# A fused attention and expert kernel: the next batch's keys split three steps sooner, and a new hand-over to the experts

## The chip, the cores and the metric

The kernel runs on one core of a Trainium2 chip. TensorE (PE) does the matrix products, VectorE (DVE) and ScalarE (ACT) prepare their operands and empty their sums, GpSimd (POOL) issues the row scatters, and SyncE (SP) issues the loads. The metric is the device time of one execution in microseconds, the median of several runs.

## The reference

`u`, `v` are 8 x 2496 x 256, `z` is 8 x 2496 x 64, and there are 8 experts with a hidden width of 1024. Everything is float32.

```python
scores = (1.0 / S) * np.matmul(z, z.transpose(0, 2, 1))     # per batch, S = 2496
attn = np.maximum(scores, 0.0) ** 2
x = (u * np.matmul(attn, v)).reshape(N, D)                  # N = 19968 tokens, D = 256
logits = x @ w_gate + modality_bias[modality_id]
e_idx = np.argmax(logits, axis=1)                           # one expert per token
gate_w = softmax(logits)[arange(N), e_idx]
out[mask_e] = gate_w * (np.maximum(x[mask_e] @ w1[e], 0.0) @ w2[e])
```

## The kernel before, in words

**Precision.** Every float32 operand of a product is split into a high part (rounded to the format that PE takes) and a low part (operand minus high), and the product is the sum of three: high x high, high x low, low x high. ACT or DVE rounds the high parts (`zm` L220, `vh` L234, `ah` L280, `hh` L954); DVE alone subtracts for the low parts (`zm` L225, `vl` L240, `al` L289, `hl` L955).

**Attention.** Each batch has five chunks of queries (four of 512 and one of 448) and twenty blocks of 128 keys. A step `g` is one chunk of queries with two blocks of keys: 10 steps to a chunk, 50 to a batch, 400 in all. `scores` (L265) puts two blocks' products into the tile `s`, which exists once (two PSUM banks); ACT takes `s` through a relu into `r` (L267) and squares it (L273); `high` and `low` split it; `weigh` (L305) adds its product with `v` to the sums `acc`. Scores run four steps ahead of `weigh` once the pipe is full, so `scores(g)` stands on PE in step `g - 4`. The fifth chunk's keys of a batch that starts at step `g0` are first read by `scores(g0 + 8)`, hence in step `g0 + 4`. When a chunk of queries ends, ACT copies half of its sums out (`evacuate_low`, L347), DVE adds the other half (`evacuate_high`, L351), PE turns the result into rows (`make_rows`, tile `po`, L363), DVE multiplies by `u` (`take_rows`, L373), and 32 DVE products per chunk make the gate's logits (L385).

**What sets the order.** PE, ACT, DVE and POOL run their instructions in the order in which the program writes them. A planner writes it: `at(g, f)` puts a task right behind step `g`; `queue(g, end, pieces)` lets pieces wait from step `g` on until an account of ACT's and DVE's time has room, and at step `end` at the latest; a second piece follows one step later. Loads go through SP's queue, in which an instruction that waits for a buffer holds up those behind it. `z` is loaded into three raw buffers (`zr`), which the subtraction at L225 frees.

**Hand-over and experts.** The tokens of the early batches are already sorted into expert queues in memory (`scatter`, L496 and L498), so four expert tiles of 512 tokens can run before the last tokens are routed. In a tile, `up` makes eight slices of the hidden layer (tile `ph`, six matmuls, L950), ACT and DVE split each (`hh`, `hl`), and `down` (L963, L964) multiplies slice `f - 2` with the second weights behind slice `f`; slices 6 and 7 follow at the tile's end. `finish` empties the four sums with ACT (`part2`, L978) and DVE (`y`, L980). The rest of the last batch's work (turning the last chunk, its logits, the routing of its 12 late columns, the plan for all other tiles) is hung into the first four tiles by the table `between[tile][slice]`. `route_count` (L462) is a product on PE that reads `cnt` (L453) of `route_places`. Phase one's PSUM holds `s` in its first two banks and six banks that `acc`, `po` and others share; phase two's pools lie over the same banks in the order in which they are opened, and a tile waits for the users of the bank under it.

Of the kernel before, what the change touches and what calls it, by code (L numbers as in the profile page):

```python
# [15 lines left out]
P = 128  # L16
# [10 lines left out]
def tile_attention_moe(ctx: ExitStack, tc: tile.TileContext, u, v, zt, mid, wg, mb, w1, w2, out):  # L27
# [11 lines left out]
    nc = tc.nc  # L39
# [138 lines left out]
    nc.sync.dma_start(out=brow, in_=mb.rearrange("(o m) e -> o m e", o=1).broadcast_to([P, 2, E]))  # L178
    mod = [small.tile([P, B, NCOL, 1], F32, name=f"mod{i}") for i in range(2)]

    def load_modality():
        mi = raw.tile([P, B, NCOL, 2], I32, tag="mi", name="mi")
# [73 lines left out]
    def scores(g):  # L256
# [4 lines left out]
        for n, (kl, ql) in enumerate(((0, 1), (1, 0), (0, 0))):  # L261
            for t in range(2):
                k = 2 * i + t
                lhs = Z[b, k // J][halves[t], kl, (k % J) * P:(k % J + 1) * P]
                nc.tensor.matmul(out=s[:, t, :w], lhsT=lhs, rhs=mv[halves[t], ql, :w], start=n == 0, stop=n == 2)  # L265
# [391 lines left out]
    for b in range(B):  # L657
        g0 = b * per
        if b:
            for c in range(NCH):  # L660
# [4 lines left out]
                queue(gz, g0 + 2 * c - 5, act(0.6, prep_z_high, b, c), dve(0.7, prep_z_low, b, c))  # L665
                queue(gv, g0 + 2 * c - 2, act(1.05, prep_v_high, b, c), dve(1.25, prep_v_low, b, c))
        for c in range(NCH):
# [4 lines left out]
            for h in reversed(range(KD)):  # L672
                queue(g + NI, g, dve(0.7, evacuate_high, b, c, h))
            if b < B - 1 or c < NCH - 1:
                at(g + NI, make_rows, b, c)
# [159 lines left out]
    with tc.manual_schedule(engines={ET.PE, ET.Activation, ET.DVE, ET.Pool}):  # L835
# [88 lines left out]
        assert not tasks  # L924
        waiting += [(end, g, p) for g in sorted(due) for end, p in due[g]]
# [5 lines left out]
    ph2 = ctx.enter_context(ExitStack())  # L931
    bank.update(pool=ph2.enter_context(tc.tile_pool(name="ps_m", bufs=2, space=PSUM, reuse_waits="tile")), tag="m")
# [3 lines left out]
    ps_h = ph2.enter_context(tc.tile_pool(name="ps_h", bufs=2, space=PSUM, reuse_waits="tile"))  # L936
# [95 lines left out]
    for n in range(LGN):  # L1032
        between[0][1 + n * (KF - 1) // LGN].append(lambda n=n: logits(B - 1, NCH - 1, n))
    planning = plan()
    slots = [(n, f) for n in range(EARLY) for f in range(KF)]
    late = slots[KF:]
    for (n, f), pieces in zip(late, ((route_logits, route_exp), (route_places,), (route_count,), (route_slots, route_gates))):
        between[n][f] += [lambda p=p: p(B - 1, LATE) for p in pieces]
    for k, (n, f) in zip(range(LATE.start, NCOL), late[4:]):
        between[n][f].append(lambda k=k: scatter(B - 1, k))  # L1040
    for n, f in late[3:8]:
        between[n][f] += [lambda: next(planning, None)] * 2
    n, f = late[7]
# [65 lines left out]
```

## Time and profile before

| what | value |
|---|---|
| time, median of 3 runs | 2329.91 us (2325.26 to 2331.11) |
| the profiled execution's own time | 2333.17 us |
| its span, first to last instruction | 2330.9 us |
| TensorE busy | 2280.6 us, 98% |
| VectorE busy | 1758.5 us, 75% |
| ScalarE busy | 1588.7 us, 68% |
| mean granted TensorE clock | 0.990 |

The span is what the trace covers; the execution's own time has 2.27 us around it. A granted clock of 1.0 is 2.4 GHz and 0.5 is 1.2 GHz. Busy shares are averages over the attention phase (to about 1387 us) and the expert tiles behind it.

### The profile page before, as it was taken

The numbers are of one execution on the slowest core, as the hardware profiler recorded it, in microseconds if no ns is written. First come the engines' busy times: TensorE is split into PE (matmuls) and PEld (weight loads), VectorE is DVE, ScalarE is ACT, GpSimd is POOL, SyncE is SP. The second block draws the span as 40 slices with busy tenths as digits, with TensorE's granted clock in tenths as the row PEclk, the third lists the DMA queues.
The fourth block names the chain that finished last, engine by engine and source line by source line (L and its number), as shares of the span: only waits on it lengthen the run. The fifth ranks groups of instructions, "written<-read, shape, count | busy, mean of one in ns | idle before, by whom it ended". The sixth has DMA issues, their size and how long they took to land.

```text
span 2330.9 us, 44748 instructions
## 1 busy us (share of the span) xinstructions
PE 2280.6 (98%) x17220; PEld 2069.5 (89%) x17220; DVE 1758.5 (75%) x4539; ACT 1588.7 (68%) x1967; POOL 366.3 (16%) x350
## 2 busy tenths in 40 slices
PE   9999999999999999999999999999999999999996
PEld 7888998998998998998998987888888888888885
DVE  6879988988988888988888987555656565656563
ACT  7888887888887887888888862454545454545453
POOL 0000210210210220220210412221211111111211
PEclk9999999999999999999999999999999999999998
DMA  9602112112112112112110122343434343434340
GB/s 299 221 28 67 47 48 67 45 48 75 38 52 70 40 51 69 40 59 61 51 40 30 62 90 80 128 154 118 161 111 162 112 162 112 160 116 156 124 144 24
DMA packets 101790, 216.88 MB, mean 93 GB/s; under 512 B 15488, under 2 KB 63104, under 8 KB 96704
## 3 DMA queue, kind: packets, MB, share of 16 engines
q1 hardware_dynamic: 86432, 172.61, 22.5%
q0 software_dynamic: 15136, 41.34, 4.8%
q8 instruction: 136, 2.23, 0.4%
q14 instruction: 86, 0.70, 0.1%
HBM read 168.36 MB, written 62.32 MB: 99 GB/s over the span
## 4 chain that ended last, share of the span: by engine, by line
PE 89%; DVE 6%; issue 2%; ACT 2%; DMA 0%; POOL 0%; DVEq 0%; ACTq 0%; POOLq 0%
PE acc L305 40%; PE ph L950 18%; PE po L963 12%; PE s L265 11%; PE po L964 6%; DVE spare L385 2%; DVE al L289 1%; PE pt L794 1%; PE po L363 1%; ACT r L267 1%; ACT r L273 0%; DVE ah L280 0%; DVE x L373 0%; DVE x L351 0%; DVE hl L955 0%
## 5 line engine op out<-in xcount | busy, mean ns | idle before, releaser
L267 ACT ACTIVATE r<-s 128x1024 f32<-128x1024 f32 (+1 forms) x400 | 403.5, 1009 | 224.8 <-PE s L265 219.0
L289 DVE TENSOR_TENSOR al<-r,ah 128x1024 fp32r<-128x1024 f32 (+1 forms) x360 | 431.1, 1198 | 127.7 <-ACT ah L280 112.2
L305 PE MATMUL acc<-ah,vh 64*128 64x512 f32 (+1 forms) x3120 | 474.4, 386 | 0.9 <-DVE ah L280 0.9
L305 PE MATMUL acc<-ah,vl 64*128 64x512 f32 (+1 forms) x3120 | 466.9, 385 | 0.0
L305 PE MATMUL acc<-al,vh 64*128 64x512 f32 (+1 forms) x3120 | 463.4, 383 | 0.0
L385 DVE SCALAR_TENSOR_TENSOR spare<-x,wgb 128x256 f32<-128x256 f32 x1280 | 462.4, 421 | 1.2
L954 ACT ACTIVATE hh<-ph 128x512 fp32r<-128x512 f32 (+1 forms) x320 | 189.7, 593 | 391.1 <-PE ph L950 377.7
L963 PE MATMUL po<-w,hh 128*128 128x512 f32 x1264 | 454.2, 394 | 0.0
L950 PE MATMUL ph<-xh,w 128*128 128x512 f32 (+1 forms) x1280 | 448.1, 396 | 3.6 <-DVE x L351 3.1
L273 ACT ACTIVATE r<-r 128x1024 f32<-128x1024 f32 (+1 forms) x400 | 416.2, 1040 | 3.5
L955 DVE SCALAR_TENSOR_TENSOR hl<-ph,hh 128x512 fp32r<-128x512 f32 (+1 forms) x320 | 219.1, 685 | 264.2 <-ACT hh L954 260.7
L265 PE MATMUL s<-zm 64*128 64x512 f32 (+1 forms) x2400 | 372.5, 390 | 21.9 <-DVE zm L225 19.2
L305 PEld LDWEIGHTS acc<-ah,vh 64*128 64x128 f32 x3120 | 363.5, 186 | 18.7 <-ACT x L347 1.7
L305 PEld LDWEIGHTS acc<-ah,vl 64*128 64x128 f32 x3120 | 362.1, 186 | 15.6
L305 PEld LDWEIGHTS acc<-al,vh 64*128 64x128 f32 x3120 | 363.3, 185 | 14.1
L498 POOL DMA_INDIRECT xs<-x,sloti x160 | 204.8, 1280 | 1063.4 <-DVE x L496 967.4
L964 PE MATMUL po<-w,hl 128*128 128x256 f32 x1264 | 354.4, 280 | 3.3 <-DVE hl L955 3.3
L265 PEld LDWEIGHTS s<-zm 64*128 64x128 f32 x2400 | 270.3, 186 | 37.4 <-DVE zm L225 23.0
L280 ACT CAST ah<-r 128x1024 fp32r<-128x1024 f32 (+1 forms) x292 | 297.1, 1017 | 0.0
L950 PEld LDWEIGHTS ph<-xh,w 128*128 128x128 f32 x1280 | 240.4, 188 | 60.2 <-DVE x L351 3.5
L963 PEld LDWEIGHTS po<-w,hh 128*128 128x128 f32 x1264 | 238.1, 188 | 55.5
L982 POOL DMA_INDIRECT out_dram<-y,ids x158 | 154.1, 975 | 727.6 <-DVE y L980 702.9
(138 smaller groups left out, 1972.0 us busy)
## 6 DMA issues: line engine op xcount, KB each, us to landing
w<-w1s SPq DMA_DIRECT2D x37, 1024.0 KB
w<-w2s SPq DMA_DIRECT2D x37, 1024.0 KB
xg<-xs SPq DMA_DIRECT2D x39, 516.0 KB
vr<-in_v_dram SPq DMA_DIRECT2D x32, 512.0 KB
ut<-in_u_dram SPq DMA_DIRECT2D x32, 512.0 KB
zr<-in_zt_dram SPq DMA_DIRECT2D x40, 256.0 KB
w1s<-in_moe_w_dram SPq DMA_DIRECT2D x8, 1024.0 KB
w2s<-in_moe_w_dram SPq DMA_DIRECT2D x8, 1024.0 KB
```

The source lines that it names most:

```text
L265: nc.tensor.matmul(out=s[:, t, :w], lhsT=lhs, rhs=mv[halves[t], ql, :w], start=n == 0, stop=n == 2)
L267: nc.scalar.activation(out=r[:, :, :w], in_=s[:, :, :w], func=AF.Relu, scale=INV)
L273: nc.scalar.square(out=a[:, :, :w], in_=a[:, :, :w])
L280: copy(out=ah[:, :, :w], in_=st_a[g][:, :, :w])
L289: nc.vector.tensor_tensor(out=al[:, :, :w], in0=a[:, :, :w], in1=ah[:, :, :w].bitcast(F32), op=ALU.subtract)
L305: nc.tensor.matmul(out=acc[b, c][r][dh][:, :w], lhsT=V[b, k // J][y][halves[r], k % J, dh * P:(dh + 1) * P], rhs=x[halves[r], k % 2, :w], ...
L385: nc.vector.scalar_tensor_tensor(out=spare[:, k % 2, :], in0=x[:, j, 0:D], scalar=1.0, in1=wgb[:, e, :], op0=ALU.mult, op1=ALU.mult, accum ...
L498: nc.gpsimd.indirect_dma_start(out=xs, out_offset=bass.IndirectOffsetOnAxis(ap=RT[b]["sloti"][:n, k:k + 1], axis=0), in_=x[:n, j, :], in_o ...
L950: nc.tensor.matmul(out=ph, lhsT=lhs, rhs=rhs[:, k, :], start=n == 0, stop=n == 3 * KD - 1)
L955: nc.vector.scalar_tensor_tensor(out=hl, in0=ph, scalar=0.0, in1=hh.bitcast(F32), op0=ALU.max, op1=ALU.subtract)
L963: nc.tensor.matmul(out=po[j], lhsT=hh[:, s], rhs=both, start=f == 0, stop=False, skip_group_check=True)
L964: nc.tensor.matmul(out=po[j][:, 0:D], lhsT=hl[:, s], rhs=w[:, 0, :], start=False, stop=f == KF - 1, skip_group_check=True)
```

## The change

Five edits:

- `prep_z_high` and `prep_z_low` of a later batch have to be written three steps sooner (`g0 + 2 * c - 8` in place of `- 5`).
- The last chunk's `evacuate_high` leaves the planner's queue and is written right behind the last step, ahead of what is left in that queue.
- The pool of `ph` is opened first in phase two, so its two banks are those that `s` had; the general pool `m` gets the next two, which `ph` had.
- In the table `between`, the last logits are spread over slices 1 to 6 in place of 1 to 7; `route_logits` goes from the second tile's slice 0 to the first tile's slice 7, `route_places` from slice 1 of the second tile to slice 0, `route_count` and `route_slots` stay at slices 2 and 3, the scatters stay, and the plan's eight pieces run one to a slice from the second tile's slice 4 in place of two to a slice from its slice 3. The load of the next weights, which needs the plan, goes from slice 7 of the second tile to slice 4 of the third.
- The gate's bias (`brow`) is loaded behind the first `z` and `v` and not ahead of them, and the very first scores take the product of the high parts first.

```diff
-    nc.sync.dma_start(out=brow, in_=mb.rearrange("(o m) e -> o m e", o=1).broadcast_to([P, 2, E]))
     def load_modality():
+        nc.sync.dma_start(out=brow, in_=mb.rearrange("(o m) e -> o m e", o=1).broadcast_to([P, 2, E]))
...
-        for n, (kl, ql) in enumerate(((0, 1), (1, 0), (0, 0))):
+        for n, (kl, ql) in enumerate(((0, 1), (1, 0), (0, 0)) if g else ((0, 0), (0, 1), (1, 0))):
...
-                queue(gz, g0 + 2 * c - 5, act(0.6, prep_z_high, b, c), dve(0.7, prep_z_low, b, c))
+                queue(gz, g0 + 2 * c - 8, act(0.6, prep_z_high, b, c), dve(0.7, prep_z_low, b, c))
...
-            for h in reversed(range(KD)):
-                queue(g + NI, g, dve(0.7, evacuate_high, b, c, h))
             if b < B - 1 or c < NCH - 1:
+                for h in reversed(range(KD)):
+                    queue(g + NI, g, dve(0.7, evacuate_high, b, c, h))
...
         assert not tasks
+        for h in reversed(range(KD)):
+            evacuate_high(B - 1, NCH - 1, h)
         waiting += [(end, g, p) for g in sorted(due) for end, p in due[g]]
...
+    ps_h = ph2.enter_context(tc.tile_pool(name="ps_h", bufs=2, space=PSUM, reuse_waits="tile"))
     bank.update(pool=ph2.enter_context(tc.tile_pool(name="ps_m", bufs=2, space=PSUM, reuse_waits="tile")), tag="m")
...
-    ps_h = ph2.enter_context(tc.tile_pool(name="ps_h", bufs=2, space=PSUM, reuse_waits="tile"))
...
-        between[0][1 + n * (KF - 1) // LGN].append(lambda n=n: logits(B - 1, NCH - 1, n))
+        between[0][1 + n * (KF - 2) // LGN].append(lambda n=n: logits(B - 1, NCH - 1, n))
...
-    slots = [(n, f) for n in range(EARLY) for f in range(KF)]
-    late = slots[KF:]
-    for (n, f), pieces in zip(late, ((route_logits, route_exp), (route_places,), (route_count,), (route_slots, route_gates))):
+    slots = [(n, f) for n in range(EARLY) for f in range(KF)][KF - 1:]
+    for k, pieces in ((0, (route_logits, route_exp)), (1, (route_places,)), (3, (route_count,)), (4, (route_slots, route_gates))):
+        n, f = slots[k]
         between[n][f] += [lambda p=p: p(B - 1, LATE) for p in pieces]
-    for k, (n, f) in zip(range(LATE.start, NCOL), late[4:]):
+    for k, (n, f) in zip(range(LATE.start, NCOL), slots[5:]):
         between[n][f].append(lambda k=k: scatter(B - 1, k))
-    for n, f in late[3:8]:
-        between[n][f] += [lambda: next(planning, None)] * 2
-    n, f = late[7]
+    for n, f in slots[5:13]:
+        between[n][f].append(lambda: next(planning, None))
+    n, f = slots[13]
     between[n][f] += [lambda: fetch_weights(0)]
```

The changed file is two lines longer, so from the hand-over on its line numbers are two higher (L957 of the changed kernel is L955 of the one before).

ScalarE where the second batch begins, right behind the copies of the first batch's last sums (`zm` is the fifth chunk's high part). Before:

```order
L347 COPY x<-acc 128x448 x2
L234 CAST vh<-vr 128x1024
L267 ACTIVATE r<-s 128x1024
L273 ACTIVATE r<-r 128x1024
L267 ACTIVATE r<-s 128x1024
L280 CAST ah<-r 128x1024
L273 ACTIVATE r<-r 128x1024
L234 CAST vh<-vr 128x1024
L267 ACTIVATE r<-s 128x1024
L273 ACTIVATE r<-r 128x1024
L220 CAST zm<-zr 128x512
```

Now:

```order
L347 COPY x<-acc 128x448 x2
L234 CAST vh<-vr 128x1024
L220 CAST zm<-zr 128x512
L267 ACTIVATE r<-s 128x1024
L273 ACTIVATE r<-r 128x1024
L267 ACTIVATE r<-s 128x1024
L273 ACTIVATE r<-r 128x1024
L234 CAST vh<-vr 128x1024
L267 ACTIVATE r<-s 128x1024
```

The rounding of `zm` moved up past three relus, three squares and a rounding of `v`, and the rounding of `ah` (L280) that stood there left ScalarE for VectorE. The other six batch starts read alike.

VectorE at the same place, from a low part of `v` on (`zm` is the fifth chunk's low part). Before:

```order
L240 TENSOR_TENSOR vl<-vr,vh 128x1024
L289 TENSOR_TENSOR al<-r,ah 128x1024
L373 TENSOR_TENSOR x<-po,ut 128x4x2x64 x2
L280 CAST ah<-r 128x1024
L289 TENSOR_TENSOR al<-r,ah 128x1024
L385 SCALAR_TENSOR_TENSOR spare,lg<-x,wgb 128x256 x6
L240 TENSOR_TENSOR vl<-vr,vh 128x1024
L289 TENSOR_TENSOR al<-r,ah 128x1024
L385 SCALAR_TENSOR_TENSOR spare,lg<-x,wgb 128x256 x2
L225 TENSOR_TENSOR zm<-zr,zm 128x512
```

Now:

```order
L240 TENSOR_TENSOR vl<-vr,vh 128x1024
L225 TENSOR_TENSOR zm<-zr,zm 128x512
L280 CAST ah<-r 128x1024
L289 TENSOR_TENSOR al<-r,ah 128x1024
L373 TENSOR_TENSOR x<-po,ut 128x4x2x64 x2
L280 CAST ah<-r 128x1024
L289 TENSOR_TENSOR al<-r,ah 128x1024
L385 SCALAR_TENSOR_TENSOR spare,lg<-x,wgb 128x256 x2
L240 TENSOR_TENSOR vl<-vr,vh 128x1024
```

The subtraction of `zm` moved up past three of `al`, one of `vl`, eight logits, the two of `take_rows` and one rounding.

VectorE at the hand-over, from the last two low parts of the first weights on (`x<-acc` is `evacuate_high`). Before:

```order
L774 TENSOR_TENSOR w_0_18681<-w_0_18681 128x4x256 x2
L496 COPY x<-side 128x2
L385 SCALAR_TENSOR_TENSOR spare,lg<-x,wgb 128x256 x2
L351 TENSOR_TENSOR x<-acc,x 128x448 x2
L955 SCALAR_TENSOR_TENSOR hl<-ph,hh 128x512 x2
```

Now:

```order
L774 TENSOR_TENSOR w_0_18681<-w_0_18681 128x4x256 x2
L351 TENSOR_TENSOR x<-acc,x 128x448 x2
L496 COPY x<-side 128x2
L385 SCALAR_TENSOR_TENSOR spare,lg<-x,wgb 128x256 x2
L957 SCALAR_TENSOR_TENSOR hl<-ph,hh 128x512 x2
```

The two additions moved ahead of one copy and two logits. PE's order is the same in both kernels.

## Rows read from the trace of the kernel before

**Rows 1.** The page: busy times, and one of the costliest groups (busy, mean ns).
```profile
PE 2280.6 (98%) x17220; PEld 2069.5 (89%) x17220; DVE 1758.5 (75%) x4539; ACT 1588.7 (68%) x1967; POOL 366.3 (16%) x350
...
L385 DVE SCALAR_TENSOR_TENSOR spare<-x,wgb 128x256 f32<-128x256 f32 x1280 | 462.4, 421 | 1.2
```

**Rows 2.** TensorE's waits: us in total, times, longest.
```profile
PE s L265 <- DVE zm L225: 19.2, 8, 2.7
PE po L964 <- DVE hl L955: 3.3, 2, 2.9
```

**Rows 3.** Timeline of TensorE, 34 to 201 us: start, duration, work, [idle before <- releaser].
```profile
34.38 0.74 PE L265 MATMUL s<-zm 64*128 64x512 f32 x4 [0.58 <-DVE zm L225]
...
201.03 0.73 PE L265 MATMUL s<-zm 64*128 64x512 f32 x4 [2.24 <-DVE zm L225]
```

**Rows 4.** Windows of 7 us behind three z waits; PEclk stands right behind POOL.
```profile
201.03:208.03 7.00, 7.00 (x48) 5.61 (x50) 3.60 (x7) 3.29 (x4) 0.00 (x0) 0.76 0.41 133
373.43:380.43 7.00, 7.00 (x36) 5.58 (x38) 3.60 (x7) 2.10 (x3) 0.00 (x0) 0.57 0.40 118
...
1063.88:1070.88 7.00, 7.00 (x62) 5.75 (x64) 4.40 (x8) 4.88 (x5) 0.00 (x0) 1.00 0.44 135
```

**Rows 5.** Timeline of VectorE, 189 to 209 us.
```profile
189.66 1.22 DVE L240 TENSOR_TENSOR vl<-vr,vh 128x1024 fp32r<-128x1024 f32 x1
...
200.28 0.69 DVE L225 TENSOR_TENSOR zm<-zr,zm 128x512 fp32r<-128x512 f32 x1
...
208.83 1.23 DVE L289 TENSOR_TENSOR al<-r,ah 128x1024 fp32r<-128x1024 f32 x1 [4.09 <-ACT ah L280]
```

**Rows 6.** Timeline of ScalarE, 186 to 195 us.
```profile
186.83 1.05 ACT L267 ACTIVATE r<-s 128x1024 f32<-128x1024 f32 x1
...
194.76 0.60 ACT L220 CAST zm<-zr 128x512 fp32r<-128x512 f32 x1
```

**Rows 7.** Timeline of TensorE, 187 to 188 us.
```profile
187.93 0.50 PE L265 MATMUL s<-zm 64*128 64x512 f32 x1
```

**Rows 8.** Timeline of TensorE at the hand-over and in the first two tiles.
```profile
1389.77 0.79 PE L950 MATMUL ph<-xh,w 128*128 128x512 f32 x1 [3.13 <-DVE x L351]
...
1392.63 0.94 PE L363 MATMUL po<-ident,x 64*128 64x64 f32 x16
...
1413.12 0.28 PE L964 MATMUL po<-w,hl 128*128 128x256 f32 x1
...
1423.28 0.27 PE L462 MATMUL pc<-cnt,below 128*128 128x8 f32 x1 [1.94 <-DVE cnt L453]
...
1444.09 0.38 PE L964 MATMUL po<-w,hl 128*128 128x256 f32 x1 [2.89 <-DVE hl L955]
```

**Rows 9.** Windows of 7 us behind the hand-over's three long waits, of which one stands.
```profile
1389.77:1396.77 7.00, 7.00 (x37) 5.30 (x38) 2.11 (x4) 1.36 (x3) 0.00 (x0) 0.76 0.29 94
```

**Rows 10.** Timeline of VectorE at the hand-over.
```profile
1386.00 2.35 DVE L774 TENSOR_TENSOR w<-w 128x1024 fp32r<-128x1024 f32 x2
...
1389.10 1.15 DVE L351 TENSOR_TENSOR x<-acc,x 128x448 f32<-128x448 f32 x2
```

**Rows 11.** Timeline of VectorE, the first tile's last low part.
```profile
1411.97 0.69 DVE L955 SCALAR_TENSOR_TENSOR hl<-ph,hh 128x512 fp32r<-128x512 f32 x1 [0.26 <-ACT hh L954]
```

**Rows 12.** Timeline of TensorE at the start.
```profile
6.33 1.35 PE L265 MATMUL s<-zm 64*128 64x512 f32 x6
```

**Rows 13.** Timeline of VectorE at the start.
```profile
5.41 0.69 DVE L225 TENSOR_TENSOR zm<-zr,zm 128x512 fp32r<-128x512 f32 x1 [3.68 <-ACT zm L220]
```

**Rows 14.** Timeline of SP: a load of z, and the load of weights that needs the plan.
```profile
162.37 0.33 SPq L215 DMA_DIRECT2D zr<-in_zt_dram  x1
...
1444.56 0.34 SPq L750 DMA_DIRECT2D w<-w1s  x1
```

**Rows 15.** Window of 4 us behind that load; DMA share and GB/s are last.
```profile
1456.00:1460.00 4.00, 4.00 (x22) 3.40 (x21) 1.53 (x4) 0.62 (x2) 1.08 (x2) 1.00 0.16 55
```

**Rows 16.** Timeline of ScalarE: the first use of those weights.
```profile
1476.41 1.04 ACT L770 CAST w<-w 128x1024 fp32r<-128x1024 f32 x1
```

## The prediction

> **What bounds the kernel now.** I read the page first. TensorE is busy 98% of the span, no other engine over 75% [rows 1], so only what TensorE waits for, or runs at half clock, can be won. TensorE's waits come next: the largest is scores (L265) waiting for VectorE's low part of z (L225), eight times and 19.2 us, and layer two's matmul (L964) waits 3.3 us for hl [rows 2]. TensorE's timeline places them. One of the eight is the 0.58 us at 34.38 in the first batch; the other seven are one at each later batch's start, of 2.24 us at the first and of 2.71 to 2.74 us at the six others, 18.6 us in all [rows 2, 3]. At each it is the scores that read the fifth chunk's keys.
>
> The windows behind these seven waits show a second price. In the 7 us behind the first wait TensorE was granted 0.76 of full speed, so it ran at 1.2 GHz for part of it, and 7 x (1 - 0.76) = 1.7 us of work was lost. Three others are like it (0.76 to 0.78), the second one lost 7 x 0.43 = 3.0 us, and the last two read 1.00 and lost nothing [rows 4]. Together 6.5 + 3.0 = 9.5 us.
>
> VectorE's timeline says why z is late: the subtraction at 200.28 stands at the end of a queue that VectorE works off without a gap, while the low part of v at 189.66 stood eleven microseconds before. Behind it VectorE has nothing to do for 4.09 us before 208.83 [rows 5]. So the batch start is a matter of order, not of VectorE's sum of work.
>
> The hand-over has the other waits: 3.13 us before the first expert matmul at 1389.77, for the last sums; 1.94 us before route_count at 1423.28, for cnt; 2.89 us (3.3 with a second) at 1444.09, for hl behind the plan [rows 2, 8]. The 7 us behind each of the three read 0.76, as in the one shown: 1.7 us lost each [rows 9].
>
> **z three steps sooner.** No instruction is added. By the order of VectorE the subtraction now stands right behind the low part of v of 189.66, so it starts at 189.66 + 1.22 = 190.9, when the scores need it at 201.03 - 2.24 = 198.8: seven microseconds to spare [rows 3, 5]. Gain: 18.6 us of waits and the 9.5 us of half clock behind them, 28.1 us. What is late next: on VectorE everything between the new and the old place moves back by 0.69 us, and by as much again for the rounding of ah that comes over from ScalarE; the 4.09 us gap takes both.
>
> On ScalarE the rounding (0.60 us [rows 6]) now stands ahead of a relu that is itself just in time: that relu runs from 186.83 to 187.88, and the next scores, which need its tile s, start at 187.93 with TensorE already there [rows 6, 7]. Queued behind the rounding are this relu and its square; TensorE waits for the relu. ScalarE's instructions overlap by about 0.1 us, so the relu ends 0.53 us later and TensorE waits 0.53 us, at seven starts 3.7 us. Bounds: nothing, or the whole 0.60 and a little, 4.5 us. I take no fall of the clock behind so short a wait: the shortest wait above with one behind it is 1.94 us. Were there one behind each, it would be seven times 1.7 us (a rival below). Net of this part: 28.1 - 3.7 = 24.4 us.
>
> On SP, the load of z for the batch after next now stands ahead of one load of u and one of v. It waits for the same L225, which now comes earlier, so the two behind it are not held.
>
> The 9.5 us hold for this execution, and the Trainium skill, "TensorE: Matmul & The Clock Gate" (section "What's actually happening"), says that the number of slow matmuls differs between runs of one kernel. By that rule the term lies between 0 and seven full falls, 11.8 us, and the sum between 26 and 38 us. The rows agree as far as they go: seven equal waits, and two without a fall.
>
> **Last sums first, other banks for layer one.** The first expert matmuls waited for the bank of a sum that VectorE emptied at 1389.10, behind a copy and two logits. Now they write where s was, which ScalarE left long before, and can start at 1389.77 - 3.13 = 1386.64. They took 1392.63 - 1389.77 = 2.86 us at half clock [rows 8], so 1.4 us at full: done at 1388.1. The transposes behind them need both additions, which VectorE now starts when its weights' low parts end (1386.00 + 2.35 = 1388.35) and finishes 1.15 us later, at 1389.5 [rows 10]. So a wait of 1.4 us stays, for another matmul, and the transposes start 3.1 us sooner than 1392.63. What was left of the half clock behind 1392.63 is 0.3 us: 3.4 us won. Bounds: 1.7 us if the clock falls behind the 1.4 us too; 4.8 us if the remaining wait went as well, which the order excludes.
>
> **Routing and plan in other slices.** cnt is now made one slice before it was, with route_count where it was. A slice is six matmuls of layer one (1.4 us) and eight of layer two, by estimate 2.8 us, more than the 1.94 us that were missing: 1.94 + 1.7 = 3.6 us won. The plan's eight pieces get eight slices instead of five, so no hl stands behind two of them: 3.3 + 1.7 = 5.0 us won. New cost: all 32 logits now stand ahead of the first tile's last hl, where 28 did. Four at 462.4 / 1280 = 0.36 us [rows 1] are 1.4 us. That hl had idled 0.26 us before 1411.97, and ended 0.46 us before the matmul that reads it at 1413.12 [rows 8, 11]: 0.7 us of cover, so TensorE waits 0.7 us there (0 to 1.4). Then the exponentials stand ahead of ScalarE's four part2 copies; both come after the tile's last matmuls and cost TensorE nothing that it does not already lose there. The next weights' load needs the plan: issued at 1444.56, done by about 1456, when the DMA share is back to 0.16, used at 1476.41 [rows 14 to 16]. It stays at about that time and its use comes 12 us sooner: still eight to spare. Hand-over: 3.4 + 3.6 + 5.0 - 0.7 = 11.3 us.
>
> **z first.** Nothing. z comes one issue sooner and the first scores no longer need the low part, but that part was done at 6.10, and TensorE is busy with its warming matmuls until 6.33 [rows 12, 13]. Without that cover it would be worth 0.5 to 1.2 us.
>
> **Sum.** 24.4 + 11.3 = 35.7 us off the span of 2330.9: 2295.2, and with the 2.27 us around it 2297.5. The profiled execution (2333.17) lies 3.3 us above the median of the runs shown (2329.91). If that is an offset of the profile, the changed kernel's median is 2329.91 - 35.7 = 2294.2; if those runs only had fewer falls of the clock, which then are gone anyway, 2297.5. I take the middle, 2296.
>
> **Rivals.** (a) ScalarE's queue at the batch start costs more than the rounding: a relu late by a further whole instruction, 1.05 us [rows 6], is seven times 1.05 = 7.4 us: 2303. For it: that relu has no spare. Against it: ScalarE's next relus wait for TensorE.
> (b) The clock also falls behind the eight shorter waits: 8 x 1.7 = 13.6 us: 2309. Against it: falls are seen behind 1.94 us and more, and even two waits of 2.7 us had none [rows 4]. The Trainium skill, same page (section "A second HAM failure mode: psum-queue depth-cycling"), says that short idle spells between groups of matmuls can make the clock swing; by that rule this is the time. No row here shows it behind a wait under a microsecond.
> (c) VectorE, with its logits closer together, is late in the first two tiles and gives the 11.3 us back as waits for hl: 2307. For it: such a wait cost 5.0 us before. Against it: the same work begins 3 us sooner.
> (d) The change does not do what it says, the low part of z still comes last: only the hand-over, 2318. The order speaks against it.
> (e) Slower: the rounding of z now stands in front of the relu, and if z has not landed, ScalarE's queue stops there. Place: the relu of 186.83; price: every microsecond seven times; it decides from 35.7 / 7 = 5.1 us at each start. Against it: the load of that z is issued at 162.37 [rows 14], over 24 us before. 2330 and more, say 2340.
>
> **How the numbers follow.** Chances: forecast 0.71, (a) 0.09, (b) 0.06, (c) 0.05, (d) 0.03, gains that cancel to within 0.3% 0.03, (e) 0.03. 0.3% is about what a measurement of this kernel can tell from no change (7 us). Faster: 0.71 + 0.09 + 0.06 + 0.05 + 0.03 = 0.94; same 0.03; slower 0.03. Low end: no new waits (4.4 us) and the seven falls full (2.3 us more) give 2294.2 - 6.7 = 2287.5, so 2287. High end: (a) and most of (c), 2306. Outside lie (b), (d), the cancelled case and (e), 0.15.
>
> **What would show it.** Right: TensorE has no wait for L225 behind the first batch, instead seven of some 0.5 us for the relu L267; the granted clock behind the batch starts is 1.00; the first expert matmul comes at once, with a 1.4 us wait at the transposes; no wait at route_count; one of under 1.4 us for the first tile's last hl. Wrong, if waits for L267 of over a microsecond stand at the batch starts, if the clock falls there without a long wait, or if tiles one and two show waits for hl.

## The result, and the profile after

| kernel | median, us | lowest to highest | runs |
|---|---|---|---|
| before | 2327.59 | 2323.52 to 2331.11 | 4 |
| after | 2294.47 | 2293.02 to 2295.52 | 4 |

The ratio of the times is 0.986, with a 95% interval of 0.9844 to 0.9876: faster by 33 us, 1.5 us under the forecast of 2296 and inside its range. The profiled execution after took 2293.02 us, over a span of 2290.8 us, at a mean granted clock of 0.997.

The page of the changed kernel, its busy times and the group of scores (the last column is the idle time ahead of them):

```profile
PE 2263.6 (99%) x17220; PEld 2022.7 (88%) x17220; DVE 1758.0 (77%) x4540; ACT 1587.7 (69%) x1966; POOL 367.1 (16%) x350
...
L265 PE MATMUL s<-zm 64*128 64x512 f32 (+1 forms) x2400 | 363.6, 387 | 4.9 <-ACT r L267 4.4
```

TensorE's waits in the changed kernel: us in total, times, longest.

```profile
PE s L265 <- ACT r L267: 4.4, 12, 1.1
PE po L363 <- DVE x L351: 1.6, 2, 1.3
...
PE s L265 <- DVE zm L225: 0.6, 1, 0.6
PE po L966 <- DVE hl L957: 0.5, 1, 0.5
```

The wait for the low part of z, 19.2 us in eight [rows 2], is down to the first batch's 0.6. Seven of the twelve waits for the relu (L267) are new and stand at the batch starts. Of the two waits at L363 one is at the hand-over; the other, 0.35 us at 220.22 where the second batch's first chunk is turned, is new too. VectorE's work as a whole is unchanged (1758.0 us against 1758.5). TensorE's timeline of the changed kernel, with the second batch's first scores, three batch starts, the last scores and the hand-over:

```profile
169.42 0.39 PE L265 MATMUL s<-zm 64*128 64x512 f32 x2
...
185.83 0.50 PE L265 MATMUL s<-zm 64*128 64x512 f32 x2 [0.22 <-ACT r L267]
...
354.64 0.50 PE L265 MATMUL s<-zm 64*128 64x512 f32 x2 [0.25 <-ACT r L267]
...
522.86 0.51 PE L265 MATMUL s<-zm 64*128 64x512 f32 x2 [0.24 <-ACT r L267]
...
1345.16 0.36 PE L265 MATMUL s<-zm 64*128 64x448 f32 x1
...
1358.18 0.50 PE L952 MATMUL ph<-xh,w 128*128 128x512 f32 x1
...
1361.09 0.59 PE L363 MATMUL po<-ident,x 64*128 64x64 f32 x12 [1.25 <-DVE x L351]
...
1382.00 0.39 PE L966 MATMUL po<-w,hl 128*128 128x256 f32 x1 [0.48 <-DVE hl L957]
...
1384.31 0.39 PE L952 MATMUL ph<-xh,w 128*128 128x512 f32 x1
...
1390.19 0.17 PE L462 MATMUL pc<-cnt,below 128*128 128x8 f32 x1
...
1407.83 0.39 PE L952 MATMUL ph<-xh,w 128*128 128x512 f32 x1
```

The first expert matmul (1358.18) and route_count (1390.19) carry no wait any more [rows 8]. Four rows of the timeline of the kernel before that the accounts below need (the second batch's first scores, a z wait, the last scores, the third tile's first matmul):

```profile
172.04 0.39 PE L265 MATMUL s<-zm 64*128 64x512 f32 x2
...
547.01 1.22 PE L265 MATMUL s<-zm 64*128 64x512 f32 x4 [2.74 <-DVE zm L225]
...
1373.56 0.36 PE L265 MATMUL s<-zm 64*128 64x448 f32 x1
...
1447.96 0.39 PE L950 MATMUL ph<-xh,w 128*128 128x512 f32 x1
```

The windows behind the new batch starts, in the changed kernel (PEclk, the granted clock, right behind POOL; a window that reads under 1.00 is called a fall of the clock below), against 0.57 to 1.00 before [rows 4]:

```profile
185.83:192.83 7.00, 7.00 (x62) 5.76 (x64) 6.79 (x13) 6.13 (x6) 0.00 (x0) 1.00 0.35 112
354.64:361.64 7.00, 7.00 (x62) 5.77 (x64) 6.90 (x16) 6.13 (x6) 0.00 (x0) 1.00 0.34 93
```

From these rows the two profiled executions can be laid side by side. The second batch's first scores come 172.04 - 169.42 = 2.6 us sooner, the third tile's first matmul 1447.96 - 1407.83 = 40.1 us sooner, and behind it nothing differs (the spans differ by 40.1 too). Of the 37.5 us between, 25.8 lie ahead of the last scores (1373.56 before, 1345.16 after, so 28.4 us sooner, less the 2.6), which leaves 11.7 for the hand-over.

### The profile page after: what moved, and what is told of

Read it like the earlier page. It is cut to its first block, busy times and chain, and to the rows that moved or that the text cites. A ratio compares the mean times of both kernels' runs of the same rounds, so it can differ in the third digit from the quotient of the medians.

```text
span 2290.8 us, 44756 instructions
## 1 busy us (share of the span) xinstructions
PE 2263.6 (99%) x17220; PEld 2022.7 (88%) x17220; DVE 1758.0 (77%) x4540; ACT 1587.7 (69%) x1966; POOL 367.1 (16%) x350
## 4 chain that ended last, share of the span: by engine, by line
PE 92%; DVE 3%; ACT 2%; issue 2%; DMA 0%; POOL 0%; ACTq 0%; POOLq 0%; DVEq 0%
PE acc L305 42%; PE ph L952 18%; PE po L965 12%; PE s L265 11%; PE po L966 6%; DVE spare L385 1%; PE pt L794 1%; ACT r L267 1%; PE po L363 1%; ACT r L273 0%; DVE al L289 0%; ACT vh L234 0%; ACT x L347 0%; DMA out_dram<-y,ids 0%; DVE hl L957 0%
## 5 line engine op out<-in xcount | busy, mean ns | idle before, releaser
L267 ACT ACTIVATE r<-s 128x1024 f32<-128x1024 f32 (+1 forms) x400 | 403.4, 1008 | 198.3 <-PE s L265 187.6
L305 PE MATMUL acc<-ah,vh 64*128 64x512 f32 (+1 forms) x3120 | 465.7, 384 | 0.9 <-DVE ah L280 0.9
L305 PE MATMUL acc<-ah,vl 64*128 64x512 f32 (+1 forms) x3120 | 458.5, 383 | 0.0
L305 PE MATMUL acc<-al,vh 64*128 64x512 f32 (+1 forms) x3120 | 456.5, 382 | 0.1
L957 DVE SCALAR_TENSOR_TENSOR hl<-ph,hh 128x512 fp32r<-128x512 f32 (+1 forms) x320 | 219.1, 685 | 255.3 <-ACT hh L956 251.8
L305 PEld LDWEIGHTS acc<-ah,vh 64*128 64x128 f32 x3120 | 349.8, 184 | 27.5 <-ACT x L347 1.6
L305 PEld LDWEIGHTS acc<-al,vh 64*128 64x128 f32 x3120 | 350.1, 184 | 23.1 <-DVE al L289 0.5
L305 PEld LDWEIGHTS acc<-ah,vl 64*128 64x128 f32 x3120 | 347.3, 184 | 24.6
L265 PE MATMUL s<-zm 64*128 64x512 f32 (+1 forms) x2400 | 363.6, 387 | 4.9 <-ACT r L267 4.4
L280 ACT CAST ah<-r 128x1024 fp32r<-128x1024 f32 (+1 forms) x291 | 296.0, 1017 | 0.0
L265 PEld LDWEIGHTS s<-zm 64*128 64x128 f32 x2400 | 260.3, 185 | 24.8 <-ACT r L267 7.5
```

The source lines that it names most:

```text
L267: nc.scalar.activation(out=r[:, :, :w], in_=s[:, :, :w], func=AF.Relu, scale=INV)
L280: copy(out=ah[:, :, :w], in_=st_a[g][:, :, :w])
L305: nc.tensor.matmul(out=acc[b, c][r][dh][:, :w], lhsT=V[b, k // J][y][halves[r], k % J, dh * P:(dh + 1) * P], rhs=x[halves[r], k % 2, :w], ...
L957: nc.vector.scalar_tensor_tensor(out=hl, in0=ph, scalar=0.0, in1=hh.bitcast(F32), op0=ALU.max, op1=ALU.subtract)
```

## Experiments

The kernel before was run beside each group of four (e1 to e4, e5 to e8, e9 to e12) and took 2325.6 to 2327.5 us in the median, single runs of it 2323.5 to 2334.2. The changed kernel was run beside the first table's kernel before only, so between medians of different groups a difference of one or two us shows nothing by itself; there the traces decide. e3 has ten runs, e12 five, the others four.

| run | edit | median, us | lowest to highest |
|---|---|---|---|
| after | all five edits | 2294.47 | 2293.02 to 2295.52 |
| e1 | z edit alone | 2306.74 | 2305.84 to 2307.42 |
| e2 | three hand-over edits alone | 2314.15 | 2313.51 to 2317.14 |
| e3 | start edit alone | 2325.68 | 2323.20 to 2333.77 |
| e4 | z two steps sooner, alone | 2306.43 | 2303.80 to 2306.59 |
| e5 | all but the start edit | 2294.34 | 2294.09 to 2294.74 |
| e6 | after, weights' low parts behind the sums | 2293.79 | 2292.47 to 2295.21 |
| e7 | after, logits spread as before | 2294.97 | 2293.55 to 2296.35 |
| e8 | after, with e4, e6 and e7 | 2292.79 | 2292.56 to 2295.12 |
| e9 | after, old banks | 2296.34 | 2295.85 to 2296.61 |
| e10 | after, last sums in the queue | 2296.50 | 2295.25 to 2298.13 |
| e11 | after, old slices | 2301.60 | 2300.51 to 2302.46 |
| e12 | after, with e4 and e6 | 2291.42 | 2291.32 to 2293.63 |

### The parts alone: e1, e2, e3

e1 is the kernel before with this edit:

```diff
-                queue(gz, g0 + 2 * c - 5, act(0.6, prep_z_high, b, c), dve(0.7, prep_z_low, b, c))
+                queue(gz, g0 + 2 * c - 8, act(0.6, prep_z_high, b, c), dve(0.7, prep_z_low, b, c))
```

> The first edit alone, z three steps sooner. My theory: the seven waits for the low part of z go, seven waits of 0.5 us for the relu take their place, no fall of the clock at the batch starts: 24 to 26 us faster than before, some 2303, with the hand-over's three waits and their falls as before. Rival (a): a later relu gives 17. Rival (b), the clock falls behind the short waits too: 14. If the parts were not independent (the start edit warms the clock for what follows), it would differ from the 25.8 us that the batch starts gained in the whole change.

It measured 0.9914 of before (0.9897 to 0.993), 20.8 us by the medians, less than the 24 to 26 expected; in its trace the stretch from the second batch's first scores to the last scores is 25.7 us shorter than in the profiled execution of before, as in the whole change. The two differ because that execution of before had more clock falls than most: its mean granted clock was 0.990, that of the 13 runs of before beside e1 0.991 to 0.994, and e2 shows the same batch starts with fewer falls. e2 is the kernel before with the early additions, the new banks and the new slices:

```diff
-            for h in reversed(range(KD)):
-                queue(g + NI, g, dve(0.7, evacuate_high, b, c, h))
...
+        for h in reversed(range(KD)):
+            evacuate_high(B - 1, NCH - 1, h)
...
+    ps_h = ph2.enter_context(tc.tile_pool(name="ps_h", bufs=2, space=PSUM, reuse_waits="tile"))
     bank.update(pool=ph2.enter_context(tc.tile_pool(name="ps_m", bufs=2, space=PSUM, reuse_waits="tile")), tag="m")
...
-        between[0][1 + n * (KF - 1) // LGN].append(lambda n=n: logits(B - 1, NCH - 1, n))
+        between[0][1 + n * (KF - 2) // LGN].append(lambda n=n: logits(B - 1, NCH - 1, n))
...
```

> The three edits of the hand-over alone. My theory: 11 to 12 us faster than before (some 2317), independent of the batch starts: two waits remain, about 1.25 us at the transposes and 0.5 us at the first tile's last low part, no fall of the clock behind the last scores. Rival: part of the 11.7 us came from a last batch that begins earlier or on a faster clock; then less than 9 us.

It measured 0.995 (0.9933 to 0.9966), 13.4 us, an interval that holds the trace's 11.7 too. The hand-over in its trace is the changed kernel's to within 0.1 us (waits of 1.25 and 0.48 us), so it doesn't need the earlier batches. Its batch starts have the old order and the old waits; its timeline and windows there:

```profile
372.89 0.50 PE L265 MATMUL s<-zm 64*128 64x512 f32 x2 [2.73 <-DVE zm L225]
...
543.68 0.50 PE L265 MATMUL s<-zm 64*128 64x512 f32 x2 [2.73 <-DVE zm L225]
```

```profile
200.50:207.50 7.00, 7.00 (x48) 5.90 (x50) 3.60 (x7) 3.28 (x4) 0.00 (x0) 0.76 0.40 131
372.89:379.89 7.00, 7.00 (x62) 5.77 (x64) 4.42 (x8) 4.89 (x5) 0.00 (x0) 1.00 0.41 125
```

The waits are the same 2.73 us, yet the clock fell behind the first of the seven alone; in before it fell behind five. A batch from wait to wait took 543.68 - 372.89 = 170.79 us here and 547.01 - 373.43 = 173.58 us in before [rows 4]. So the fall at 373 us, whose window read 0.57, cost 2.8 us where the prediction had 3.0.

e3 is the kernel before with the start edit:

```diff
...
     def load_modality():
+        nc.sync.dma_start(out=brow, in_=mb.rearrange("(o m) e -> o m e", o=1).broadcast_to([P, 2, E]))
...
+        for n, (kl, ql) in enumerate(((0, 1), (1, 0), (0, 0)) if g else ((0, 0), (0, 1), (1, 0))):
```

> The start edit alone. My forecast for it was nothing. Rival, from the trace of the changed kernel: first scores 0.9 us sooner and no fall of the clock at 10.8 us, so 2.6 us faster. If the 2.6 us were a matter of when the clock rose in that one execution, the granted clock of the start will differ between executions of one kernel, and the median gains about 1 us (0.9 us of an earlier first matmul) or nothing.

It measured 1.0002 (0.999 to 1.0013): nothing that can be measured, as forecast, though the interval would hide 2 us either way. Its trace shows first scores at 5.61 us in place of 6.33 and no clock fall at the start, so by the trace alone it would have looked like a gain of 2.5 us. e5 settles that below.

### What the rounding ahead of the relu costs: e4

e4 is e1 with one step less; ScalarE then rounds z behind the square that follows the tight relu (the one that the prediction called just in time):

```diff
-                queue(gz, g0 + 2 * c - 8, act(0.6, prep_z_high, b, c), dve(0.7, prep_z_low, b, c))
+                queue(gz, g0 + 2 * c - 7, act(0.6, prep_z_high, b, c), dve(0.7, prep_z_low, b, c))
```

> z two steps sooner in place of three, nothing else changed. The rounding then stands behind the tight relu, not ahead of it, and the low part of z behind the first take_rows, still microseconds ahead of its use. My theory says that the remaining 0.5 us waits are the price of standing ahead of that relu: they go, and this is 28 us faster than before, 3 to 4 us faster than the first edit alone. Rival: the relu is tight for another reason, then both are equal; or the low part comes late behind take_rows, then waits for it of up to a microsecond stand at the batch starts.

It measured 0.9909 (0.9892 to 0.9925), 2306.43 us against e1's 2306.74: no difference by the medians, where 3 to 4 us were expected. In its profiled run the clock also fell behind the wait of the first expert matmul (0.78 over the 7 us behind it) and in e1's it did not (1.00), which hides part of the difference in this pair. The traces tell the two apart. TensorE's timeline in e1, from the transposes ahead of the tight relu on:

```profile
355.97 0.88 PE L363 MATMUL po<-ident,x 64*128 64x64 f32 x16
357.10 0.50 PE L265 MATMUL s<-zm 64*128 64x512 f32 x2 [0.25 <-ACT r L267]
...
525.34 0.50 PE L265 MATMUL s<-zm 64*128 64x512 f32 x2 [0.25 <-ACT r L267]
...
559.10 0.67 PE L363 MATMUL po<-ident,x 64*128 64x64 f32 x14
```

And in e4, with its weight loads (PEld) behind it:

```profile
355.32 0.22 PE L363 MATMUL po<-ident,x 64*128 64x64 f32 x1
...
355.94 0.50 PE L265 MATMUL s<-zm 64*128 64x512 f32 x1
355.99 0.22 PE L363 MATMUL po<-ident,x 64*128 64x64 f32 x1
...
524.01 0.49 PE L265 MATMUL s<-zm 64*128 64x512 f32 x1
```

```profile
558.18 0.26 PEld L363 LDWEIGHTS po<-ident,x 64*128 64x128 f32 x5 [0.47 <-DVE x L351]
```

From the first transpose to the scores it is 1.13 us in e1 and 0.62 in e4: the rounding costs 0.51 us at that spot, as predicted. The idle time shown, 0.25, is less: in e4 the scores start at 355.94, before the last of the transposes (355.99, 0.22 us long), while in e1 idle time counts only from the end of the last one. But a whole batch is 525.34 - 357.10 = 168.24 us in e1 and 524.01 - 355.94 = 168.07 in e4. The other 0.3 us are given back some 34 us later: at the turn of the batch's first chunk e4's transposes wait 0.47 us for VectorE's addition (L351), while e1, which comes later, finds it done and shows no wait. From the second batch's first scores to the last scores e1 takes 1175.78 us and e4 1174.29: against e4 all seven roundings together cost 1.5 us.

Against the order of before it looks different. The fourth batch has no fall in e1, e2 and e4; its three stretches, from its first scores to those behind the tight relu, on to its first transposes, and on to the next batch's first scores, in us:

| run | to the scores behind the relu | to the transposes | to the next batch |
|---|---|---|---|
| e2 (old order, z wait of 2.73 us) | 16.01 | 36.85 | 117.94 |
| e1 (three steps sooner) | 16.52 | 33.76 | 117.96 |
| e4 (two steps sooner) | 15.89 | 34.17 | 117.99 |

Against e2, e1 loses 0.5 us at the relu and never gets it back, but the z wait that went had lengthened its stretch by 3.1 us, not by the 2.73 that it showed as idle time. e4 keeps the 0.5 us and loses 0.4 to VectorE in the second stretch. So without the delay at the relu VectorE's addition is the next limit.

### The start: e5

e5 is the whole change with the start as in before:

```diff
...
     def load_modality():
-        nc.sync.dma_start(out=brow, in_=mb.rearrange("(o m) e -> o m e", o=1).broadcast_to([P, 2, E]))
...
-        for n, (kl, ql) in enumerate(((0, 1), (1, 0), (0, 0)) if g else ((0, 0), (0, 1), (1, 0))):
+        for n, (kl, ql) in enumerate(((0, 1), (1, 0), (0, 0))):
```

> All edits but the start's. The traces so far: the three kernels with the old start show the clock at half for 3.4 us from some 10 us on, the two with the new one do not, and their first scores stand 0.7 to 0.9 us sooner. If the start edit is what keeps the clock up, this is 2.3 to 2.6 us slower than the whole change: some 2297. If that was chance (my forecast of nothing), it is within 1 us of 2294.5, and its own trace may show the start without the fall.

It measured 2294.34 us, 0.9858 of before where the changed kernel has 0.986: the same. Windows of 7 us behind the first relu wait of the start, first in e5 (old start), then in e9 (new start; its second line is for later):

```profile
8.45:15.45 7.00, 6.07 (x48) 4.39 (x50) 5.22 (x6) 6.12 (x8) 0.00 (x0) 1.00 1.00 350
```

```profile
8.54:15.54 7.00, 6.14 (x38) 4.63 (x40) 5.23 (x6) 5.06 (x6) 0.00 (x0) 0.76 0.96 352
1362.90:1369.90 7.00, 7.00 (x44) 5.59 (x45) 4.38 (x13) 1.80 (x3) 0.97 (x1) 1.00 0.28 97
```

The old start went without a fall here and the new one had it, so the edit doesn't decide the fall. (What goes with it over all the traces is told in the last section.) What the edit does is seen in TensorE's timeline at the start: the 22 warming matmuls and the first scores, in e5 and then in e9.

```profile
1.47 4.49 PE L839 MATMUL warm<-zeros 64*128 64x512 f32 x22 [1.47 <-DVE zeros L94]
6.37 0.50 PE L265 MATMUL s<-zm 64*128 64x512 f32 x2 [0.41 <-DVE zm L225]
```

```profile
1.47 5.06 PE L839 MATMUL warm<-zeros 64*128 64x512 f32 x22 [1.47 <-DVE zeros L94]
6.33 0.62 PE L265 MATMUL s<-zm 64*128 64x512 f32 x2
```

The warming matmuls take 5.06 us in e9, as in before, and 4.49 in e5; in after it was 4.12. Where they end early, the old order waits for the low part of z (0.41 us in e5), while the new one starts at 5.42 us in after. Where they end late, both orders start at 6.33 (before [rows 12], e9). So the cover that the prediction named is there in some executions and not in others, and the edit is worth between nothing and a microsecond, as the prediction bounded it.

### The three hand-over edits undone one by one: e9, e10, e11

e9 is the whole change with the old order of the pools:

```diff
-    ps_h = ph2.enter_context(tc.tile_pool(name="ps_h", bufs=2, space=PSUM, reuse_waits="tile"))
     bank.update(pool=ph2.enter_context(tc.tile_pool(name="ps_m", bufs=2, space=PSUM, reuse_waits="tile")), tag="m")
...
+    ps_h = ph2.enter_context(tc.tile_pool(name="ps_h", bufs=2, space=PSUM, reuse_waits="tile"))
```

> The whole change with the banks of layer one as before, so the first expert matmul again waits for a bank of the last sums. My theory: it waits for the first of the two additions, some 2.3 us, and the transposes then follow without a wait: 1.1 us slower than the whole change, or 2.5 if the clock falls behind that wait. Rival: only the place of the wait moves, no difference in the time of the second tile's start.

TensorE's timeline in e9 at the first expert matmul and at the transposes:

```profile
1362.90 0.51 PE L952 MATMUL ph<-xh,w 128*128 128x512 f32 x1 [2.31 <-DVE x L351]
...
1364.50 0.40 PE L363 MATMUL po<-ident,x 64*128 64x64 f32 x6
```

The wait came back with 2.31 us, the transposes follow without one, and from the last attention matmul to the last transpose it is 1.07 us more than in after, as expected. The clock stayed up behind it (1.00 in the second window above). The median is 1.9 us above the changed kernel's, in another group; the profiled run has a fall at its start besides, so only the 1.07 us is put down to the banks.

e10 is the whole change with the last additions left in the planner's queue:

```diff
...
-        for h in reversed(range(KD)):
-            evacuate_high(B - 1, NCH - 1, h)
```

> The whole change with the last additions left in the planner's queue, behind one copy and two logits. My theory: the first expert matmul still starts at once, and the wait at the transposes grows from 1.25 by the 0.85 us of these three to 2.1: 0.8 to 0.9 us slower. Rival: the first tile is bound by VectorE's sum of work, then the wait at its last low part shrinks by as much and the second tile starts at the same time.

TensorE's timeline in e10 at the transposes and at the second tile, and the window behind the wait:

```profile
1362.38 0.40 PE L363 MATMUL po<-ident,x 64*128 64x64 f32 x6 [2.07 <-DVE x L351]
...
1386.29 0.39 PE L950 MATMUL ph<-xh,w 128*128 128x512 f32 x1
```

```profile
1362.38:1369.38 7.00, 7.00 (x39) 5.76 (x40) 3.94 (x13) 1.20 (x2) 0.00 (x0) 0.76 0.27 91
```

The wait grew to 2.07 us as expected, and the clock fell behind it, which was not expected. From the transposes to the second tile it is 1386.29 - 1362.38 = 23.91 us, against 1384.31 - 1361.09 = 23.22 in after, though the wait at the first tile's last low part is gone. Between the last attention matmul and the second tile the loss is 1.5 us in all, by the medians 2.0. The second tile starts later, so the rival's forecast failed; but the last wait did shrink, as the rival said, and with the fall in between this run doesn't show what the order alone would cost there.

e11 is the whole change with the table of slices as in before:

```diff
-        between[0][1 + n * (KF - 2) // LGN].append(lambda n=n: logits(B - 1, NCH - 1, n))
+        between[0][1 + n * (KF - 1) // LGN].append(lambda n=n: logits(B - 1, NCH - 1, n))
...
-    for n, f in slots[5:13]:
-        between[n][f].append(lambda: next(planning, None))
+    for n, f in late[3:8]:
+        between[n][f] += [lambda: next(planning, None)] * 2
...
```

> The whole change with routing and plan in their old slices. My theory: waits of 1.9 us for cnt and of 2.9 and 0.6 us behind the plan come back, the 0.76 us at the first tile's last low part goes: 4.7 us slower, and up to 8.1 with the clock falling behind two of them, as it did in all traces that had these waits. Rival: part of the gain belongs to the earlier start of VectorE's work, then under 4.

TensorE's waits in e11, the two that came back, and the windows behind them:

```profile
PE po L966 <- DVE hl L957: 3.9, 2, 2.9
PE pc L462 <- DVE cnt L453: 1.9, 1, 1.9
```

```profile
1391.79:1398.79 7.00, 7.00 (x35) 5.95 (x36) 4.51 (x22) 1.20 (x2) 0.00 (x0) 1.00 0.01 2
1411.64:1418.64 7.00, 7.00 (x22) 5.87 (x23) 2.02 (x6) 2.19 (x5) 4.86 (x5) 0.56 0.73 248
```

The median is 7.1 us above the changed kernel's (5.6 by the two ratios to before); in the trace 8.7 us are lost between the first and the fifth tile, a little more than the bound given. The waits came back in full. The clock stayed up behind the first of them, where it fell in before, and was down for longer behind the others (0.56). The rival is out.

### Better versions: e6, e7, e8, e12

e6 moves the low parts of the first expert's second weights behind the last additions:

```diff
-        queue(G - 8 + q, G - 4 + q, act(1.05, part_weights_high, -1, q), dve(1.25, part_weights_low, -1, q))
+        lowp = dve(1.25, part_weights_low, -1, q)
+        queue(G - 8 + q, G - 4 + q, act(1.05, part_weights_high, -1, q), *[lowp] * (q < KD))
+        if q >= KD: queue(G, G, lowp)
```

> The whole change, and the last two low parts of the first expert's weights (2.35 us of VectorE) moved behind the last sums. My theory of the 1.25 us left at the transposes: VectorE stands in these two when the sums are ready. So the wait goes, 1.2 to 1.3 us faster than the whole change. Rival: the weights' low parts are then late for layer two's first products, and a wait of a microsecond or more stands there in its place: no gain or slower.

```profile
1360.21 0.40 PE L363 MATMUL po<-ident,x 64*128 64x64 f32 x6 [0.25 <-DVE x L351]
...
1363.15 0.50 PE L954 MATMUL ph<-xh,w 128*128 128x512 f32 x1 [0.64 <-DVE hl L959]
```

These rows of e6's TensorE show both theories in part: the wait at the transposes shrank to 0.25 us, and 0.64 us came up three microseconds later for the first low part `hl` (L959 here), which now stands behind the weights. The 0.48 us at the first tile's end went too. Net, the second tile starts 1.0 us sooner, measured from the first scores; the median, 2293.79, is 0.7 under after, within the spread of the runs. In the time that the weights took in the changed kernel VectorE now runs two logits ahead of the last sums (1357.84 and 1358.18 us).

e7 is the whole change with the old spread of the logits:

```diff
-        between[0][1 + n * (KF - 2) // LGN].append(lambda n=n: logits(B - 1, NCH - 1, n))
+        between[0][1 + n * (KF - 1) // LGN].append(lambda n=n: logits(B - 1, NCH - 1, n))
```

> The whole change, with the last logits spread over seven slices as before. My theory of the wait at the first tile's last low part (0.48 us idle, 0.76 us lost): the four logits that came ahead of it. So it goes, 0.7 to 0.8 us faster than the whole change, and route_count still finds cnt done, as the whole change made cnt 1.2 us ahead of it. Rival: the four logits only move the delay, and a wait of up to 1.4 us stands at the next tile's first low part or at route_count.

```profile
1388.10 0.50 PE L952 MATMUL ph<-xh,w 128*128 128x512 f32 x1 [0.83 <-DVE hl L957]
```

This row of e7's TensorE is the second tile: the wait at the first tile's end is gone, and one of 0.83 us stands here in its place. The third tile starts 0.15 us later than in after, measured from the first scores. The rival held: those four logits can be moved, but VectorE's queue around the first tile's end is full, and someone waits.

e8 has the three diffs of e4, e6 and e7 on top of the whole change, e12 those of e4 and e6.

> The whole change with z two steps sooner in place of three, the weights' last two low parts behind the last sums, and the logits spread as before. By the traces, z gives 0.2 us a batch start or 1.3, the other two 1.25 and 0.76: 3.3 us faster than the whole change, some 2291. Rival: these three meet in VectorE's queue at the hand-over and only one of the last two is seen: 2292 to 2293.

> The whole change with z two steps sooner and the weights' last two low parts behind the last sums, the logits as in the change. From the traces: 1.3 us from z, 1.0 from the weights: 2.3 us faster than the whole change, some 2292.2, and 0.8 faster than the kernel that also spread the logits as before. Rival: the wait at the first tile's last low part comes back and takes 0.5 to 0.8 of it.

e8 measured 2292.79 us, with the waits of e6 and of e7 both in its trace, so its rival held. e12 measured 2291.42 us, ratio to before 0.9843 (0.9824 to 0.9861); its waits:

```profile
PE s L265 <- ACT r L267: 2.7, 5, 1.1
...
PE ph L954 <- DVE hl L959: 1.0, 2, 0.6
...
PE po L363 <- DVE x L351: 0.6, 2, 0.4
```

It is the fastest of all, 3.0 us under the changed kernel by the medians. The ranges of their runs overlap, and 0.13% is less than a measurement can tell. By the traces, from the second batch's first scores to the third tile, it is 2.4 us shorter than the changed kernel, where 2.3 were expected.

## Why the prediction was right, step by step

**z three steps sooner**, forecast 24.4 us, in the trace 25.8.
- The seven waits, 18.6 us, are gone to the last one, as forecast. One batch without any fall went from 170.79 us (e2) to 168.24 (e1), so 2.55 us where the prediction's terms give 2.73 - 0.53 = 2.2.
- The half clock behind them, 9.5 us: right in kind. By time it was 8.8: from the second batch's first scores to the last ones e2, which lacks four of the five falls (one of them the long one), is 7.3 us shorter than before (1194.22 against 1201.52); the fifth is taken as one of the three other short ones, 1.5. The windows give the work that TensorE lost; the batch became longer by a little less.
- The relu behind the rounding, 3.7 us: the mechanism and the local price were right (0.51 us between e1 and e4, against 0.53). The step that failed is the sizing of these two terms, "18.6 us of waits" and "at seven starts 3.7 us": each was priced by itself, the wait by the idle time that the trace shows. Against the old order the 0.5 us do stay, and the wait that went was worth 3.1 us; against e4 the seven delays are worth 1.5 us, since without them VectorE's addition holds TensorE up at the first chunk's turn. By either count the gain is some 2 us more than the two terms gave. The limit at the turn is one that the prediction looked for ("What is late next") and took to be covered by the 4.09 us gap.
- Rivals (a), (b) and (d) are out: no relu wait over 0.25 us at the batch starts, and the windows behind read 1.00. (e) is out too: no wait for z's load. One ground against (b) was false all the same: falls are not only seen behind 1.94 us and more, since the start of the kernel before has one behind two waits of 1.1 and 0.9 us (last section).

**Last sums first, other banks**, forecast 3.4 us: from the last attention matmul to the last transpose it is 3.3 us in place of 6.7, so 3.4 us. The remaining wait is 1.25 us where 1.4 was forecast, no fall followed it, and its cause is the weights' low parts that VectorE is in (e6). Taken out alone, the banks are worth 1.07 us and the order 0.8 us at the transposes. The rest is put down to the clock (the six matmuls ahead of the transposes took 2.86 us in before, at half clock, and 1.60 in e9); no run has both edits out, so that is argued.

**Routing and plan in other slices**, forecast 8.6 us less a new wait of 0.7. The second tile went from 1447.96 - 1415.31 = 32.65 us (with the waits of [rows 8]) to 1407.83 - 1384.31 = 23.52, 9.1 us less. The new wait at the first tile's last low part shows 0.48 us idle and costs 0.8: from the transposes to the second tile it is 23.22 us, against 22.45 in e11, which has no such wait (1361.36 to 1383.81). The falls behind the old waits, which the prediction took as certain, are not: e1 has none behind its 3.14 us at the first expert matmul. Rival (c), VectorE late in the first two tiles, is seen in this one place only.

**z first**, forecast nothing: e3 and e5 measure nothing, within their intervals.

**The sum.** The profile shows no offset: the profiled execution after, 2293.02 us, does not lie above its runs (median 2294.47). That of before lay above its median because of its falls; its granted clock was 0.990, and runs of before near 2325 us show 0.993 to 0.994. So the reading that gave 2297.5 was the right one. Against its 35.7 us the two profiled executions differ by 2333.17 - 2293.02 = 40.15: 2.6 us at the start of this one execution (chance), 2.2 us more from the z waits and the relu, 0.4 us more from the hand-over, less 0.7 of the falls. By the right reading the forecast would have been 3.0 us above the median. That the middle, 2296, lies within 1.5 us is luck; the mechanism and most of the terms are not.

## What to carry to other kernels

Price a delay that you add by following it to the next place where its engine waits for a slower neighbour: what is lost at one spot can be given back there (0.51 us in e1 against e4 became 0.2). Price a wait that you remove by the length of its stretch and not by the idle time shown (3.1 us for 2.73). And where a queue is full, moving a piece out of the way of one consumer puts it in front of the next (e7); put it into a stretch in which the engine would idle, as e6 did with its two logits. A gain that one pair of traces shows at the clock's mercy, like the start here, needs a kernel without the edit before it is put down to the edit.

## What the runs showed of the hardware

Whether the clock falls behind a wait is not set by the length of the wait alone. Behind the 2.7 us at the batch starts it fell in four of six cases in before and in none of six in e2 (1.00 in the window at 372.89). Of the waits at the hand-over, 3.14 us in e1, 2.31 us in e9 and 1.95 us in e11 kept 1.00, 2.07 us in e10 read 0.76.

It also fell behind shorter waits than the prediction allowed for: at the start, where TensorE waits 1.1 and 0.9 us in close order, in six of the fourteen traces. The kernel before is one of the six:

```profile
8.77:15.77 7.00, 6.12 (x38) 4.65 (x40) 5.19 (x6) 5.09 (x6) 0.00 (x0) 0.76 0.99 376
```

At this place the fall goes with what TensorE did ahead of the wait. In the six (before, e1, e2, e4, e9, e12) the 22 warming matmuls took 5.06 us; in the eight others they took 4.12 to 4.77 us, and the windows read 1.00. The old start is among both, and so is the new one.

Behind the 0.25 us waits at the batch starts no fall is seen in any of the traces that have them. The Trainium skill, "TensorE: Matmul & The Clock Gate" (section "What's actually happening"), says that the number of slow matmuls differs from run to run of one kernel; the runs of before agree, with mean granted clocks from 0.990 to 0.994. What decides in a single case at the batch starts and the hand-over these runs don't show, and it stays open. For a forecast it means that the falls in one profile are a sample: the kernel before spread over 10 us in its 33 runs, and the changed one, which had no long wait left, over 2.5 in its four.
